# Retention attention and two feed-forward layers on one core: chunk 0 ahead of chunk 1, scaling on GpSimd, filler matmuls, another weight decode order

## The chip, the cores and the metric

The kernel runs on one core of a Trainium2 chip. The metric is the device time of one execution in microseconds (us), lower is better. Three runs of the kernel before gave 593.54, 595.24 and 596.46 us; the median is 595.24 us.

## What is computed

A causal attention with decay (a running state per head) feeds two feed-forward layers. All data are float32.

```python
# attention: B=2, H=8, S=768, D=64
for t in range(S):
    state = gamma * state + outer(k[t], v[t])
    y[t] = scale * q[t] @ state
x = y.transpose(0, 2, 1, 3).reshape(1536, 512)
# layer 1: w_in 512 x 2048, w_out 2048 x 512
h = x @ w_in
x = (max(h, 0) + alpha * min(h, 0)) @ w_out
# layer 2
h = x @ w_in2
p = a0 + a1*h + a2*h*h + a3*h**3
x = (p / (1 + |b0|*|h| + |b1|*h*h + 1e-6)) @ w_out2
```

## The kernel before

**Attention** goes in 12 chunks of 128 time steps, six for each batch entry. For a chunk `c`, `att_b` multiplies keys and queries of all heads into two PSUM banks (tiles `sc`, line L132), VectorE multiplies them with the decay mask into `s` (L136), and, when the chunk is not the first of its batch entry, ScalarE scales the queries by a constant per partition (L141, four instructions) and VectorE by the table `dq` (L142). `att_k` scales the keys `k` by a decay factor per head; for chunks below 8 that is eight ScalarE instructions (L120), for later ones one GpSimd instruction (L123). `att_c` computes `y` from `s` and `v` (L153), the chunk's own state `st` from the scaled `k` and `v` (L165), and adds the scaled `q` times the running state `R` (L177). Then `R` is copied or added to (L181, L183), and `y` is split into a high part `xh` (ScalarE, L187) and a low part `xl` (VectorE, L188). TensorE's instructions stand in a fixed order, and each of the other engines takes its own in the order written, so an instruction that waits holds everything behind it.

**The layers** are cut into 16 slices `m` of the hidden width and 3 blocks of 512 tokens. A step computes a hidden tile `h` with 12 matmuls (L309: high and low parts of `x` and of the weights), applies the activation, and multiplies it into four accumulator banks with 12 more (L326). Block 0 needs chunks 0 to 3, so the first hidden step stands behind chunk 3. The first sweep takes five slices, with the later chunks of the attention between its steps. PSUM gives four banks to a ring (`sc`, `h`, and from chunk 4 on `y` and `st`) and four to the accumulators; chunks 0 to 3 borrow those for `y` and `st`.

**Weights** arrive as 64-bit numbers, 512 KB for each half slice, and are decoded to a high part `wh` and a low part `wl`: ScalarE takes the absolute value (L253, "abs"), VectorE does three bit operations (L259, L263, L267, "word"), ScalarE rounds to `wh` (L278, "hi"), VectorE subtracts to get `wl` (L284, "lo"). The table `START` gives each half slice `(layer, m, 0 or 1)` a half step `t` at which its decode begins; "word", "hi" and "lo" follow at `t+1`, `t+2`, `t+3`. `SEQ`, the order of START, is also the order of loading. `half(t)` issues what is due at `t`; the eight entries of the list `order` (the attention of chunks 0 to 3) are the half steps -12 to -5.

**Loads** go out from SyncE's queue in the order written; each of them waits for the landing of the load eight places ahead of it. `load_next(depth)` loads weights until `depth` are in flight.

Of the kernel before, what the change touches and what calls it, by code (L numbers as in the profile page):

```python
# [11 lines left out]
ALU = mybir.AluOpType  # L12
# [19 lines left out]
def tile_fused(  # L32
# [34 lines left out]
    def drop(t):  # L67
        free.append(slot.pop(id(t))[0])
# [45 lines left out]
    def att_k(c):  # L114
        k = r8(att[c]["k"])
        if c % CPB < CPB - 1:
            o = 8 * (c % CPB)
            if c < 8:
                for h in range(8):
                    nc.scalar.mul(k[:, h, :], k[:, h, :], cst_sb[:, o + h:o + h + 1])  # L120
            else:
                dk = cst_sb[:, o:o + 8].unsqueeze(2)
                nc.gpsimd.tensor_tensor(out=k, in0=k, in1=dk.to_broadcast([P, 8, 64]), op=ALU.mult)  # L123

    def att_b(c, bank):
        a = att[c]
        ps = [bank(f"sc{c}_{e}") for e in range(2)]
        for j in range(NK):
            js = slice(j * P, (j + 1) * P)
            for e in range(2):  # L130
                es = slice(64 * e, 64 * e + 64)
                nc.tensor.matmul(ps[e][:, js], a["t"][es, js], a["q"][es, js], start=True, stop=True)  # L132
        a["s"] = alloc(f"s{c}")
        for e in range(2):
            es = slice(512 * e, 512 * e + 512)
            nc.vector.tensor_tensor(out=a["s"][:, es], in0=ps[e], in1=dm_sb[:, es], op=ALU.mult)  # L136
        if c % CPB > 0:
            for j in range(NK):
                js = slice(j * P, (j + 1) * P)
                o = 8 * CPB + 4 * (c % CPB) + j  # L140
                nc.scalar.mul(a["q"][:, js], a["q"][:, js], cst_sb[:, o:o + 1])  # L141
            nc.vector.tensor_tensor(out=a["q"], in0=a["q"], in1=dq_sb, op=ALU.mult)  # L142

    def att_c(c, ybank, pbank):
        a = att.pop(c)
# [72 lines left out]


    START = {}  # L220
    for k, e in enumerate(((1, 0), (0, 1), (2, 0), (3, 0), (1, 1), (4, 0))):
        START[(0,) + e] = k - 6
    START.update({(0, 0, 0): -12, (0, 2, 1): 0, (0, 3, 1): 2, (0, 4, 1): 4})
    for j, m in enumerate(B):
        START[0, m, 0], START[0, m, 1] = 6 + (17 * j) // 5, 8 + (17 * j) // 5
    for m in range(NF):
# [12 lines left out]
    def load_next(depth):  # L239
        while loaded[0] < len(SEQ) and loaded[0] - loaded[1] < depth:  # L240
            k = loaded[0]
            loaded[0] += 1
            l, m, n = SEQ[k]
            r = alloc(f"r{k}", U32)
            nc.sync.dma_start(out=r, in_=SRC[l][n][m].bitcast(U32))
            words = r.rearrange("p (f t) -> p f t", t=2)
            raw[k] = (words[:, :, 0], words[:, :, 1], r)
# [209 lines left out]
    N1 = NB * NF  # L457
    dec = {}
    for k, e in enumerate(SEQ):
        for o, nm in enumerate(("abs", "word", "hi", "lo")):  # L460
            dec.setdefault(START[e] + o, []).append((nm, k))

    NPRE = 12
# [1 line left out]
    def half(t, scalar_last=None, between=None):  # L465
        evs = dec.get(t, ())

        def each(nm):
            return [e[1] for e in evs if e[0] == nm]

        for e in each("abs"):
            w_abs(e)
        for e in each("hi"):
            w_hi(e)
        if scalar_last:
            scalar_last()
        for e in each("word"):
            w_word(e, 0)
        for e in each("lo"):
            w_lo(e)  # L480
        for e in each("word"):
            w_word(e, 1)
        if between:
            between()
        for e in each("word"):
            w_word(e, 2)
        if later and t % 2 == 0:
            split_x(*later.pop(0))
        load_next(0 if t < -9 else 4 if t < 2 * N1 else 2)

    with tc.manual_schedule():
        wt = alloc("wz")
# [3 lines left out]
        for _ in range(NWARM):  # L496
            nc.tensor.matmul(ps[:, 0:P], wz, wz, start=True, stop=True)
        nc.scalar.preload_act_table_set("natural_log_exp_and_others")
        drop(wt)
        for c in range(4):  # L500
            att_tiles(c)
        load_kq(0)
        nc.sync.dma_start(out=dm_sb, in_=dm)
        load_next(1)
        load_kq(1)
        nc.sync.dma_start(out=cst_sb, in_=cst)
        load_nv(0)
        load_kq(2)
        load_nv(1)
        nc.sync.dma_start(out=dq_sb, in_=dq)  # L510
        load_kq(3)
        load_nv(2)
        load_nv(3)
        load_next(2)
        nc.sync.dma_start(out=alpha_sb, in_=alpha)
        nc.sync.dma_start(out=ab_sb[:, 0:4], in_=pa.partition_broadcast(P))
        nc.sync.dma_start(out=ab_sb[:, 4:6], in_=pb.partition_broadcast(P))
        nc.vector.memset(bb_sb[:, 2:3], QC)

        order = [("b", 0), ("b", 1), ("c", 0), ("b", 2), ("c", 1), ("b", 3), ("c", 2), ("c", 3)]  # L520
        for n, (s, c) in enumerate(order):
            if s == "b":
                att_b(c, rbank)
                if c == 0:
                    att_k(c)
            else:
                att_c(c, abank(c % 2), abank(2 + c % 2))
                if c < 3:
                    att_k(c + 1)
                if c == 0:  # L530
                    att_load(4)
                    load_next(4)
                if c == 1:
                    att_load(5)
            if n == 6:
                nc.scalar.activation(bb_sb[:, 0:2], ab_sb[:, 4:6], AF.Abs)
                nc.scalar.mul(nalpha_sb, alpha_sb, -1.0)
            half(n - NPRE)
        att_b(4, rbank)
        att_k(4)  # L540


# [124 lines left out]
```

## Time and profile before

| | us |
|---|---|
| median of three runs (lowest, highest) | 595.24 (593.54, 596.46) |
| the profiled execution, device time | 595.47 |
| the profiled execution, span from first to last instruction | 593.7 |
| TensorE busy in the span | 580.1 |
| VectorE busy | 467.6 |
| ScalarE busy | 372.8 |
| GpSimd busy | 66.9 |
| mean granted TensorE clock, as a share of full speed | 0.988 |

PE is TensorE's matmuls, DVE VectorE, ACT ScalarE, POOL GpSimd, SPq SyncE's queue of loads. Times in rows are counted from the span's start. A PE group that reads x16 in the attention holds 8 matmuls of the program.

### The profile page before, as it was taken

What the parts mean: (1) busy time and instruction counts of PE and PEld (TensorE: products, weight loads), DVE (VectorE), ACT (ScalarE), POOL (GpSimd) and SP (SyncE); (2) the same over time, 40 slices, a digit from 0 to 9 for tenths busy, and PEclk for the clock granted to TensorE, in tenths of its full rate; (3) what the DMA queues carried; (4) which work ended last, traced back from release to release, by engine and by line L of the source; (5) the groups of instructions that cost most, each with busy time, mean ns of one, the idle gap of its engine ahead of it and who ended that gap; (6) DMA issues with size and microseconds to landing.
All of it is one profiled execution on the core that took longest, in us unless ns stands there. A gap on an engine that the chain in (4) does not pass through costs nothing.

```text
span 593.7 us, 8087 instructions
## 1 busy us (share of the span) xinstructions
PE 580.1 (98%) x3024; PEld 478.1 (81%) x3024; DVE 467.6 (79%) x736; ACT 372.8 (63%) x695; POOL 66.9 (11%) x53
## 2 busy tenths in 40 slices
PE   6988999999999999999999999999999999999997
PEld 6866778788888888888888888888888888888885
DVE  1786779767886255446998999999999989887886
ACT  3955655555655353444766687777787776776672
POOL 0001000000000000000000222232222222212220
PEclk8988999999999999999999999999999999999999
DMA  8997312223420111012453010111101100010101
GB/s 304 369 396 264 135 58 94 107 88 126 142 83 24 36 36 37 35 36 71 154 201 107 1 36 0 36 36 36 36 26 46 37 1 1 0 72 0 46 26 72
DMA packets 18760, 50.65 MB, mean 85 GB/s; under 512 B 2592, under 2 KB 2592, under 8 KB 18720
## 3 DMA queue, kind: packets, MB, share of 16 engines
q1 hardware_dynamic: 18720, 50.13, 24.0%
q8 instruction: 24, 0.39, 0.3%
q14 instruction: 16, 0.13, 0.1%
HBM read 46.97 MB, written 3.15 MB: 84 GB/s over the span
## 4 chain that ended last, share of the span: by engine, by line
PE 94%; DVE 2%; DMA 1%; ACT 1%; SPq 0%; issue 0%; ACTq 0%
PE h L309 44%; PE acc L326 43%; PE y L153 2%; PE sc L132 2%; PE y L177 2%; PE st L165 1%; DMA qk<-in_kT_dram 1%; DVE p L423 0%; ACT g L406 0%; DVE s L136 0%; DVE as L399 0%; DVE as L396 0%; DVE as L395 0%; DVE wl L284 0%; DVE z L259 0%
## 5 line engine op out<-in xcount | busy, mean ns | idle before, releaser
L309 PE MATMUL h<-xh,wl 128*128 128x512 f32 x384 | 150.6, 392 | 4.0 <-DVE wl L284 4.0
L309 PE MATMUL h<-xh,wh 128*128 128x512 f32 x384 | 150.8, 393 | 0.3 <-DVE xl L188 0.3
L309 PE MATMUL h<-xl,wh 128*128 128x512 f32 x384 | 150.2, 391 | 0.0
L326 PE MATMUL acc<-wh,g 128*128 128x512 f32 x384 | 125.9, 390 | 0.4 <-ACT g L406 0.4
L326 PE MATMUL acc<-g,wh 128*128 128x512 f32 x384 | 119.5, 393 | 0.0
L408 POOL TENSOR_TENSOR g<-as,g 128x512 fp32r<-128x512 f32 x46 | 63.4, 1377 | 455.5 <-PE acc L326 272.6
L309 PEld LDWEIGHTS h<-xh,wl 128*128 128x128 f32 x384 | 72.4, 189 | 19.8 <-DVE wl L284 4.9
L309 PEld LDWEIGHTS h<-xh,wh 128*128 128x128 f32 x384 | 72.3, 188 | 15.9 <-DVE xl L188 0.5
L326 PEld LDWEIGHTS acc<-wh,g 128*128 128x128 f32 x384 | 72.1, 188 | 16.1 <-ACT g L406 0.9
L326 PEld LDWEIGHTS acc<-g,wh 128*128 128x128 f32 x384 | 72.2, 189 | 15.7 <-issue 0.7
L309 PEld LDWEIGHTS h<-xl,wh 128*128 128x128 f32 x384 | 72.4, 189 | 15.2 <-DVE xl L188 0.2
L278 ACT CAST wh<-z 128x512 fp32r<-128x512 f32 x64 | 39.6, 618 | 56.9 <-DVE z L267 55.7
L326 PE MATMUL acc<-g,wl 128*128 128x512 f32 x192 | 75.0, 391 | 0.0
L326 PE MATMUL acc<-wl,g 128*128 128x512 f32 x192 | 74.7, 389 | 0.0
L350 DVE SCALAR_TENSOR_TENSOR np<-np,nalpha_sb 128x512 f32<-128x512 f32 x48 | 35.9, 748 | 39.9 <-ACT np L345 39.9
L344 ACT ACTIVATE np<-h 128x512 f32<-128x512 f32 x48 | 28.5, 594 | 45.1 <-PE h L309 45.1
L371 ACT ACTIVATE as<-h 128x512 f32<-128x512 f32 x48 | 28.6, 596 | 41.2 <-PE h L309 41.2
L377 DVE SCALAR_TENSOR_TENSOR as<-as,bb_sb,rr 128x512 f32<-128x512 f32 x48 | 37.9, 790 | 13.0 <-ACT rr L372 13.0
L360 DVE TENSOR_TENSOR g<-np,g 128x512 fp32r<-128x512 f32 x48 | 34.0, 708 | 17.4 <-ACT g L355 17.2
L284 DVE TENSOR_TENSOR wl<-z,wh 128x512 fp32r<-128x512 f32 x64 | 45.8, 716 | 0.0
L267 DVE SCALAR_TENSOR_TENSOR z<-r,z 128x512 uint32<-128x512 uint32 x64 | 44.1, 690 | 1.5
L263 DVE SCALAR_TENSOR_TENSOR z<-r,z 128x512 uint32<-128x512 uint32 x64 | 44.0, 688 | 1.0
(52 smaller groups left out, 753.0 us busy)
## 6 DMA issues: line engine op xcount, KB each, us to landing
r<-in_w1i_dram SPq DMA_DIRECT2D x16, 512.0 KB, 4.9
r<-in_w1o_dram SPq DMA_DIRECT2D x16, 512.0 KB, 4.2
r<-in_w2i_dram SPq DMA_DIRECT2D x16, 512.0 KB, 3.4
r<-in_w2o_dram SPq DMA_DIRECT2D x16, 512.0 KB, 3.3
qk<-in_qT_dram SPq DMA_DIRECT2D x12, 256.0 KB, 6.3
qk<-in_kT_dram SPq DMA_DIRECT2D x12, 256.0 KB, 6.0
kv<-in_kn_dram SPq DMA_DIRECT2D x12, 256.0 KB, 5.7
kv<-in_vn_dram SPq DMA_DIRECT2D x12, 256.0 KB, 5.7
```

The costliest lines, as they stand in the source:

```text
L263: nc.vector.scalar_tensor_tensor(out=zu, in0=lo, scalar=29, in1=zu, op0=ALU.logical_shift_right, op1=ALU.bitwise_or)
L267: nc.vector.scalar_tensor_tensor(out=zu, in0=hi, scalar=0x80000000, in1=zu, op0=ALU.bitwise_and, op1=ALU.bitwise_or)
L278: nc.scalar.copy(hi, Z[k])
L284: nc.vector.tensor_tensor(out=lo, in0=Z[k], in1=hi.bitcast(F32), op=ALU.subtract)
L309: nc.tensor.matmul(ps, w[:, ks], xs(hl, b, k, ALL), start=(n == 0), stop=(n == 11))
L326: nc.tensor.matmul(acc[0][k], a, c, start=(begin and n == 0), stop=(end != "" and n == 2))
L344: nc.scalar.activation(n, h, AF.Relu, scale=-1.0)
L350: nc.vector.scalar_tensor_tensor(out=p, in0=n, scalar=nalpha_sb[:, m:m + 1], in1=p, op0=ALU.mult, op1=ALU.add)
L360: nc.vector.tensor_tensor(out=gl, in0=p, in1=gh.bitcast(F32), op=ALU.subtract)
L371: nc.scalar.activation(s, h, AF.Square)
L377: nc.vector.scalar_tensor_tensor(out=s, in0=s, scalar=bb_sb[:, 1:2], in1=r, op0=ALU.mult, op1=ALU.add)
L408: eng.tensor_tensor(out=gl, in0=a, in1=gh.bitcast(F32), op=ALU.subtract)
```

## The change

The loads of `k` and `v` of chunk 0 go out ahead of the loads of chunk 1 and of the first weights. Chunk 0 is computed whole ahead of chunk 1. For chunks 0 to 3, GpSimd scales `k` (one instruction instead of eight on ScalarE) and multiplies `q` by `dq` (instead of VectorE). After the first three entries of `order`, 3, 2 and 3 matmuls on a tile of zeros (`keep_warm`) stand ahead of the next entry. `START` of the first sweep becomes regular, and the second weight's "word" and "hi" come a half step later, the latter together with its "lo".

```diff
-            if c < 8:
+            if 4 <= c < 8:
                 for h in range(8):
                     nc.scalar.mul(k[:, h, :], k[:, h, :], cst_sb[:, o + h:o + h + 1])
...
-            nc.vector.tensor_tensor(out=a["q"], in0=a["q"], in1=dq_sb, op=ALU.mult)
+            eng = nc.gpsimd if c < 4 else nc.vector
+            eng.tensor_tensor(out=a["q"], in0=a["q"], in1=dq_sb, op=ALU.mult)
...
-    for k, e in enumerate(((1, 0), (0, 1), (2, 0), (3, 0), (1, 1), (4, 0))):
-        START[(0,) + e] = k - 6
-    START.update({(0, 0, 0): -12, (0, 2, 1): 0, (0, 3, 1): 2, (0, 4, 1): 4})
+    for m in A:
+        START[0, m, 0], START[0, m, 1] = 2 * m - 9, 2 * m - 4
+    START[0, 0, 0] = -10
...
-        for o, nm in enumerate(("abs", "word", "hi", "lo")):
+        for o, nm in zip((0, 1, 2, 3) if k != 1 else (0, 2, 3, 3), ("abs", "word", "hi", "lo")):
...
-        load_next(0 if t < -9 else 4 if t < 2 * N1 else 2)
+        load_next(3 if t < -6 else 4 if t < 2 * N1 else 2)
...
         load_kq(0)
         nc.sync.dma_start(out=dm_sb, in_=dm)
-        load_next(1)
-        load_kq(1)
         nc.sync.dma_start(out=cst_sb, in_=cst)
         load_nv(0)
+        load_kq(1)
+        load_next(1)
         load_kq(2)
...
-        load_next(2)
+        load_next(3)
...
+        def keep_warm(cnt):
+            w = abank(3)("warm")
+            for _ in range(cnt):
+                nc.tensor.matmul(w[:, 0:P], wz, wz, start=True, stop=True)
+
-        order = [("b", 0), ("b", 1), ("c", 0), ("b", 2), ("c", 1), ("b", 3), ("c", 2), ("c", 3)]
+        order = [("b", 0), ("c", 0), ("b", 1), ("b", 2), ("c", 1), ("b", 3), ("c", 2), ("c", 3)]
         for n, (s, c) in enumerate(order):
+            if n in (1, 2, 3):
+                keep_warm((3, 2, 3)[n - 1])
             if s == "b":
+                att_k(c)
                 att_b(c, rbank)
-                if c == 0:
-                    att_k(c)
             else:
                 att_c(c, abank(c % 2), abank(2 + c % 2))
-                if c < 3:
-                    att_k(c + 1)
-                if c == 0:
-                    att_load(4)
-                    load_next(4)
-                if c == 1:
-                    att_load(5)
+                if c < 2:
+                    att_load(4 + c)
```

SyncE's queue at the program's start, before; `qk` holds q and the transposed k of a chunk, `kv` k and v, `r` a raw weight, and a chunk has one number for each (qk_95 and kv_96 are chunk 0, qk_97 and kv_98 chunk 1).

```order
L102 DMA qk_95<-in_qT_dram 128x512
L103 DMA qk_95<-in_kT_dram 128x512
L503 DMA dm_sb<-in_dm_dram 128x1024
L245 DMA r_106<-in_w1i_dram 128x1024
L102 DMA qk_97<-in_qT_dram 128x512
L103 DMA qk_97<-in_kT_dram 128x512
L506 DMA cst_sb<-in_cst_dram 128x72
L106 DMA kv_96<-in_kn_dram 128x512
L107 DMA kv_96<-in_vn_dram 128x512
L102 DMA qk_99<-in_qT_dram 128x512
```

The same place after the change.

```order
L102 DMA qk_95<-in_qT_dram 128x512
L103 DMA qk_95<-in_kT_dram 128x512
L503 DMA dm_sb<-in_dm_dram 128x1024
L504 DMA cst_sb<-in_cst_dram 128x72
L106 DMA kv_96<-in_kn_dram 128x512
L107 DMA kv_96<-in_vn_dram 128x512
L102 DMA qk_97<-in_qT_dram 128x512
L103 DMA qk_97<-in_kT_dram 128x512
L246 DMA r_111<-in_w1i_dram 128x1024
L102 DMA qk_99<-in_qT_dram 128x512
```

Three transfers, of the first weight and of chunk 1's q and transposed k, moved from ahead of chunk 0's k and v to behind them; from the last row shown on the same data have gone out.

GpSimd after the change, from its first compute instruction to its last one on chunk 3 (kv_96 to kv_102 are chunks 0 to 3, qk_97 to qk_101 chunks 1 to 3); before, none of these rows stands there, and the first is that of chunk 8, kv_637.

```order
L123 TENSOR_TENSOR kv_96<-kv_96,cst_sb 128x512
L123 TENSOR_TENSOR kv_98<-kv_98,cst_sb 128x512
L143 TENSOR_TENSOR qk_97<-qk_97,dq_sb 128x512
L123 TENSOR_TENSOR kv_100<-kv_100,cst_sb 128x512
L143 TENSOR_TENSOR qk_99<-qk_99,dq_sb 128x512
L123 TENSOR_TENSOR kv_102<-kv_102,cst_sb 128x512
L143 TENSOR_TENSOR qk_101<-qk_101,dq_sb 128x512
```

Seven instructions came to GpSimd, in an order that alternates keys and queries.

VectorE before, around the low part of the second input slice (wl_1_415) and behind chunk 4 (y_422); s_467, qk_274 and sc_0_457 belong to chunk 5.

```order
L183 TENSOR_TENSOR R<-R,st_431 128x256
L188 TENSOR_TENSOR xl_79<-y_422,xh_76 128x4x128
L136 TENSOR_TENSOR s_467<-sc_0_457,dm_sb 128x512
L136 TENSOR_TENSOR s_467<-sc_1_458,dm_sb 128x512
L142 TENSOR_TENSOR qk_274<-qk_274,dq_sb 128x512
L259 TENSOR_SCALAR z_367<-z_367 128x512
L284 TENSOR_TENSOR wl_1_415<-z_151,wh_1_414 128x512
```

The same stretch after; here wl_1_398 is that low part, qk_171 and y_406 are chunk 4, s_451 chunk 5.

```order
L143 TENSOR_TENSOR qk_171<-qk_171,dq_sb 128x512
L260 TENSOR_SCALAR z_350<-z_350 128x512
L285 TENSOR_TENSOR wl_1_398<-z_199,wh_1_397 128x512
L264 SCALAR_TENSOR_TENSOR z_350<-r_126,z_350 128x512
L268 SCALAR_TENSOR_TENSOR z_350<-r_126,z_350 128x512
L184 TENSOR_TENSOR R<-R,st_415 128x256
L189 TENSOR_TENSOR xl_79<-y_406,xh_76 128x4x128
L136 TENSOR_TENSOR s_451<-sc_0_441,dm_sb 128x512
```

The low part moved from behind chunk 5's mask product to ahead of it. The third input slice's low part moved likewise, from behind chunk 6's mask product to ahead of chunk 5's `xl`; these are the rows after (wl_2_462 is that low part, xl_79<-y_497 chunk 5, s_532 chunk 6).

```order
L351 SCALAR_TENSOR_TENSOR np_464<-np_464,nalpha_sb 128x512
L260 TENSOR_SCALAR z_459<-z_459 128x512
L285 TENSOR_TENSOR wl_2_462<-z_350,wh_2_461 128x512
L264 SCALAR_TENSOR_TENSOR z_459<-r_319,z_459 128x512
L361 TENSOR_TENSOR g_488<-np_464,g_488 128x512
L268 SCALAR_TENSOR_TENSOR z_459<-r_319,z_459 128x512
L189 TENSOR_TENSOR xl_79<-y_497,xh_76 128x4x128
L136 TENSOR_TENSOR s_532<-sc_0_522,dm_sb 128x512
```

Between the low part and chunk 6's mask product there now stand two word operations, an activation's low part `g` and chunk 5's `xl`.

## Rows read from the trace of the kernel before

**Rows 1.** The page, part 4: engines' shares of the chain that ended last.

```profile
PE 94%; DVE 2%; DMA 1%; ACT 1%; SPq 0%; issue 0%; ACTq 0%
```

**Rows 2.** Stretches: length, busy us of PE, PEld, DVE, ACT, POOL, clock, DMA, GB/s.

```profile
41.00:42.00 1.00, 1.00 (x3) 0.33 (x1) 1.00 (x2) 0.28 (x1) 0.00 (x0) 0.50 1.02 406
...
51.00:52.00 1.00, 1.00 (x4) 0.81 (x3) 1.00 (x3) 0.51 (x1) 0.00 (x0) 0.50 0.74 289
...
100.00:593.00 493.00, 489.29 (x2225) 403.78 (x2223) 398.17 (x620) 311.62 (x536) 63.35 (x46) 1.00 0.16 54
```

**Rows 3.** TensorE in order of time: start, us, instruction, [idle before it, releaser].

```profile
10.21 2.08 PE L132 MATMUL sc<-qk 64*128 64x128 f32 x16 [3.70 <-DMA qk<-in_kT_dram]
12.21 1.97 PE L153 MATMUL y<-s,kv 128*64 128x128 f32 x16
...
18.19 1.09 PE L177 MATMUL y<-qk,R 64*64 64x128 f32 x16
...
24.30 1.99 PE L165 MATMUL st<-kv 128*64 128x64 f32 x16
...
28.33 0.50 PE L309 MATMUL h<-xh,wh 128*128 128x512 f32 x1
...
38.69 0.50 PE L309 MATMUL h<-xh,wl 128*128 128x512 f32 x1 [2.07 <-DVE wl L284]
...
42.03 1.82 PE L153 MATMUL y<-s,kv 128*64 128x128 f32 x16
...
46.28 0.50 PE L309 MATMUL h<-xh,wh 128*128 128x512 f32 x1 [0.32 <-DVE xl L188]
...
48.92 0.50 PE L309 MATMUL h<-xh,wl 128*128 128x512 f32 x1 [1.91 <-DVE wl L284]
...
57.23 0.50 PE L309 MATMUL h<-xh,wh 128*128 128x512 f32 x1
```

**Rows 4.** VectorE in order of time, around the two waits and the GpSimd instructions.

```profile
28.58 0.42 DVE L259 TENSOR_SCALAR z<-z 128x512 uint32<-128x512 uint32 x1
...
37.02 0.68 DVE L142 TENSOR_TENSOR qk<-qk,dq_sb 128x512 f32<-128x512 f32 x1
...
42.69 0.69 DVE L267 SCALAR_TENSOR_TENSOR z<-r,z 128x512 uint32<-128x512 uint32 x1
45.53 0.69 DVE L188 TENSOR_TENSOR xl<-y,xh 128x512 fp32r<-128x512 f32 x1 [2.16 <-ACT xh L187]
46.14 1.28 DVE L136 TENSOR_TENSOR s<-sc,dm_sb 128x512 f32<-128x512 f32 x2
47.34 0.93 DVE L259 TENSOR_SCALAR z<-z 128x512 uint32<-128x512 uint32 x1
...
52.31 1.53 DVE L360 TENSOR_TENSOR g<-np,g 128x512 fp32r<-128x512 f32 x1
```

**Rows 5.** GpSimd in order of time.

```profile
46.94 1.04 POOL L123 TENSOR_TENSOR kv<-kv,cst_sb 128x512 f32<-128x512 f32 x1 [46.50 <-DMA kv<-in_kn_dram]
52.06 1.24 POOL L123 TENSOR_TENSOR kv<-kv,cst_sb 128x512 f32<-128x512 f32 x1 [4.08 <-DMA kv<-in_kn_dram]
```

**Rows 6.** ScalarE in order of time: the scaling of a chunk's k.

```profile
23.89 2.02 ACT L120 ACTIVATE kv<-kv,cst_sb 128x64 f32<-128x64 f32 x8
```

**Rows 7.** SyncE's queue in order of time: issue of k of chunks 0 and 2, and dq.

```profile
4.82 0.74 SPq L106 DMA_DIRECT2D kv<-in_kn_dram  x1
...
10.09 0.33 SPq L510 DMA_DIRECT2D dq_sb<-in_dq_dram  x1
...
11.58 0.33 SPq L106 DMA_DIRECT2D kv<-in_kn_dram  x1
```

**Rows 8.** The loads issued at 4.82, 10.09 and 11.58: KB, us to landing.

```profile
kv<-in_kn_dram SPq DMA_DIRECT2D x1, 256.0 KB, 6.1
...
dq_sb<-in_dq_dram SPq DMA_DIRECT2D x1, 256.0 KB, 4.8
...
kv<-in_kn_dram SPq DMA_DIRECT2D x1, 256.0 KB, 5.4
```

More of the change, by code (lines that the diff above doesn't have):

```diff
@@ L498, in tile_fused @@
         nc.scalar.preload_act_table_set("natural_log_exp_and_others")
-        drop(wt)
         for c in range(4):
@@ L538, in tile_fused @@
             half(n - NPRE)
+        drop(wt)
         att_b(4, rbank)
```

## The prediction

> **What bounds the kernel now.** The shares of the chain come first: 94% of it is TensorE [rows 1]. Read by stretch, this holds behind 100 us, where TensorE is busy 489.29 of 493 us at full granted clock [rows 2]; nothing that the diff touches stands there. What can be won or lost lies ahead of the fourth hidden step, which starts at 57.23 [rows 3]: from there on TensorE has its operands in time, so the end moves by what that start moves.
>
> TensorE in order of time shows what it loses there. It sits idle for 3.70 us until chunk 1's transposed k lands at 10.2, and then runs at half speed: 2.08 and 1.97 us for groups that take about 1.09 later. The state matmuls of chunk 3 take 1.99 us, because each needs its head's k from ScalarE. The second and third hidden steps stop after two matmuls for 2.07 and 1.91 us, until a low part `wl` comes from VectorE [all rows 3]. Behind each of those two waits the granted clock is 0.50, the lower level (1.2 GHz), for about 3.4 us [rows 2], and the work in it takes twice its time: some 1.7 us more for each.
>
> The profiled run took 595.47 us with a span of 593.7, 1.8 us around it; the median, 595.24, is 0.2 us below that run. I make the sum against the span and subtract the gain from the median.
>
> **Loads.** 1 MB (the first weight, chunk 1's q and transposed k) goes behind chunk 0's k and v. k lands at 4.82 + 6.1 = 10.9 now, dq at 14.9, chunk 2's k at 17.0 [rows 7, 8]. Between dq's issue and that k's stand chunk 3's q and k, and three quarter-MB landings in 2.1 us give about 0.7 us each. So 1 MB is 2.6 to 2.8 us: chunk 0's k lands at about 8.2, its v at 8.9. Everything from chunk 2 on has the same bytes ahead of it and lands when it did; chunk 1's v, the load ahead of dq, at 14.2. A second weight now stands ahead of chunk 4; counted on from dq (chunk 3's q and k, four quarter MB of k and v, two weights, chunk 4's q and k) chunk 4's transposed k lands at about 23.3, 1.4 later than before but ahead of its scores. Cost: none, as long as those scores don't start before 23.3.
>
> **Start of TensorE.** Chunk 0's first product still has the mask to wait for, then v: y0 starts at 9.0 instead of 12.21. The three fillers need 0.7 to 1.4 us and end by 7.9; they cover up to half of the idle time. Whether the clock holds over the rest I can't read from a row, so I let it fall: 0.9 us for each group of matmuls, as before. That costs little, because chunk 1's y needs its v at 14.2 and its scaled q later still.
>
> **GpSimd's seven instructions.** Each takes 1.04 to 1.24 [rows 5] where ScalarE takes 2.02 for a k [rows 6] and VectorE 0.68 for a q [rows 4]. ScalarE is rid of 8 us and chunk 3's state matmuls of their 1.3 us wait. But a VectorE instruction that came up beside a GpSimd instruction took 1.53 instead of 0.69 us and ended 0.5 us behind it, and one took 0.93 instead of 0.42, while the mask product beside the same GpSimd instruction kept its 1.28 [rows 4, 5]. So a VectorE operation on two SBUF tiles waits for GpSimd's end; one that reads PSUM does not. The Trainium skill (SBUF — State Buffer, "SBUF: two separate sides") calls this an exclusive lock for the whole instruction, and names as its victims VectorE operations with two SBUF inputs or in a two-port mode; the trace agrees with 1.53 us. Without that rule one could spread a slowdown of 0.5 us over all VectorE work under GpSimd, or let any VectorE work wait: the mask products of chunks 1 to 3 beside GpSimd would lose 0.5 us three times, and the sum would be 1.5 us worse.
>
> The chain, then: dq lands at 14.9, GpSimd's q1 ends at 16.0, the state term of chunk 1 starts at about 17.0 against 18.19. VectorE's three word operations on the first weight stand behind the mask products of chunks 1 and 2 (scores at 12.2 and 14.4) and begin at 16.7, three in 1.8 us if alone; the first passes, the second meets k2 (17.0 to 18.2), the third q2 (19.0 to 20.0), so they end at 20.7 instead of 18.5. R and chunk 1's xl stand behind them, so chunk 2's state term starts at 21.1. ScalarE's rounding of that weight waits for the words, q3's scaling stands behind the rounding, and GpSimd's q3 comes at 22.5 to 23.6; the first `wl` waits for that and R behind it: chunk 3's state term runs 24.7 to 25.8, chunk 4's scores to 26.9. The first hidden step starts at 26.9 against 28.33: **1.4 us won**.
>
> **The second hidden step.** Its `wl` stood behind chunk 5's mask product, which waits for TensorE; now it stands ahead. The 2.07 us go, and with them the low clock, which cost about 1.1 in the step and 0.7 in the y behind it (1.82 against 1.09) [rows 3]: **3.9 us won**. Before, the step began about 7.5 us behind the first one (two matmuls and the wait lie ahead of 38.69); so it begins at 34.4 and ends at 37.2, and three groups of 1.09 on chunks 5 and 6 end at 40.4. What is late next is the third step.
>
> **The third hidden step.** Its `wl` moved too, ahead of chunk 5's xl. But its first matmul needs a PSUM bank that this xl releases [the 0.32 us in rows 3], and xl stands at the end of a full queue. From the second weight's words on, VectorE did before, between 28.58 and 43.38, the same kinds of instruction in the same number as it must do now ahead of chunk 5's xl, with under 0.7 us idle [rows 4]: 14.1 us of work. It starts 1.27 us behind chunk 3's state term, as before, at 27.1, and is through at 41.3 to 41.9; xl adds 0.6. So the step starts at about 42.2, TensorE having waited 1.8 us from 40.4 on: a wait for xl in the place of the wait for wl. It then runs through; I let the clock fall as it did behind 1.91 us, so that ten matmuls and the output take what they took. Ten matmuls were left at 48.92; now they are left at about 42.6: 6.3 us in all, so the third step adds **1.0**.
>
> Sum: 1.4 + 3.9 + 1.0 = 6.3. I take off 0.3 for GpSimd's starts about 0.2 us behind a landing (46.94 against about 46.7): **6.0**. Span 587.7; against the median, 589.2. VectorE keeps its backlog and TensorE its lead behind the fourth step, since steps, loads and buffer waits all come earlier together.
>
> **Bounds.** If VectorE's words slip in between GpSimd's instructions, the 2.2 us between 18.5 and 20.7 come back, and 0.8 at the first `wl`: 9.0 won, 586.2. If the clock does not fall behind the third step's wait, 1.7 more, and by the sum alone 587.5. If each GpSimd instruction takes the 1.24 of its slower row, five of them in the chain cost 0.15 each, 0.7 less. The three runs spread by 1.5 us to each side.
>
> **Rivals.**
> First, **GpSimd holds VectorE less** than I count: 586.2. For it: four of its seven instructions fall where VectorE multiplies PSUM tiles. Against: the word operations begin just as k2 lands.
> Second, **GpSimd comes late to its first instruction.** Its first one now starts at 46.94 right behind its load [rows 5], long after the program's start, so the trace doesn't show what a first instruction at 8.2 costs. If k0 were ready at 13 instead of 9.4, chunk 0's state and all behind it shift by 3.6: the first hidden step comes 2.2 us later than before instead of 1.4 earlier, the two later steps still win 4.9, less 0.3: 2.4 won, 592.8. Past 15.4 the gain is gone. The Trainium skill (GPSIMD Engine Reference, "2.1 Instruction dispatch") gives about 6 us for the first call to a freshly loaded kernel; no row here shows it, as nothing is asked of GpSimd between its start and 46.9. By that figure, counted from the program's start, GpSimd would be ready ahead of 8.2 and lose nothing; counted from its first instruction it would be ready at about 14.
> Third, **slower: the alternating queue on GpSimd becomes the bound.** k1, q1, k2, q2, k3, q3 run in order, and q2 and q3 wait for ScalarE, which waits for VectorE, which GpSimd holds. I count 10 us for the six, 13.6 to 23.6, or 1.7 each with waits. Past 29.6 (2.7 us each) all the gain is gone, and at 3.3 each the time is 599. Against: the longest of the rows is 1.24.
> Fourth, **loads are the bound and nothing changes**: they run at 1.02 of their share at 41 [rows 2]. Against: counted on at 0.7 us a quarter MB from chunk 4's k at 23.3, all that the third and the fourth step need has landed by 36, and they start at 42 and 51. It gives 595.2.
>
> **Chances.** The forecast (587.2 to 591.2) 0.60; less hold 0.13; late GpSimd, with all gains of 1 to 4 us, 0.17 (the median of these is 592.8); slower 0.06; no change 0.04. A measurement here can tell 0.5%, 3 us. Faster by more: the forecast, less hold and a third of the late case, 0.79. Within: 0.15. Slower: 0.06. The range reaches from less hold (586.2) with a lucky 1.0 of the runs' spread, 585.2, to the late case with as much of it against me, 593.8.
>
> **What would show it.** Right: y0 at 9; no wait for `wl` in the second hidden step, which starts near 34.4; 1 to 2 us idle ahead of the third, released by xl; VectorE word operations of 1.5 us or more beside GpSimd at 17 to 21; the fourth step near 51. Wrong: GpSimd's first instruction long after its load's landing; a first hidden step later than 28.3; a new wait behind 60 us.

## The result and the profile after

The changed kernel takes 585.46 us (median of 4 runs, 585.32 to 585.79) against 595.05 of the kernel before (4 runs, 593.54 to 596.46): a ratio of 0.984, 95% interval 0.9815 to 0.9865. That is 9.6 us faster, where 6.0 were forecast; the time lies inside the range, 0.3 us above its lower end, and below 587.2, where the likeliest case ends. In the profiled execution the span is 583.5 us, 10.2 less than before, and the mean granted clock 1.00 instead of 0.988. Line numbers are one higher than before.

The shares of the chain are within a point or so of what they were [rows 1]: TensorE still bounds the kernel.

```profile
PE 93%; DVE 3%; ACT 2%; DMA 1%; issue 0%; ACTq 0%
```

Stretches of the kernel after (length, busy us of PE, PEld, DVE, ACT, POOL, clock, DMA, GB/s), to be read against [rows 2]:

```profile
12.00:13.00 1.00, 1.00 (x16) 0.88 (x16) 0.82 (x2) 0.88 (x3) 0.46 (x1) 1.00 1.05 404
...
41.00:42.00 1.00, 1.00 (x6) 0.80 (x5) 1.00 (x3) 1.00 (x3) 0.00 (x0) 1.00 1.05 418
...
51.00:52.00 1.00, 1.00 (x7) 0.82 (x5) 1.00 (x2) 0.96 (x2) 0.00 (x0) 1.00 1.04 399
...
100.00:583.00 483.00, 478.98 (x2133) 395.74 (x2132) 390.86 (x607) 307.06 (x525) 63.38 (x46) 1.00 0.16 54
```

Both stretches that ran at 0.50 are at 1.00, and so is every other microsecond of the first 60, whatever work now stands in it. In the kernel before a third stretch, from about 9.4 to 16.2 us, ran at 0.50:

```profile
12.00:13.00 1.00, 1.00 (x12) 0.79 (x10) 0.71 (x2) 1.00 (x6) 0.00 (x0) 0.50 1.04 387
```

Behind 100 us TensorE still is busy all but 4 us. So the gain lies at the start. TensorE of the kernel after in order of time (start, us, instruction, [idle before it, releaser]):

```profile
7.80 1.40 PE L154 MATMUL y<-s,kv 128*64 128x128 f32 x15
...
10.34 1.16 PE L132 MATMUL sc<-qk 64*128 64x128 f32 x16
...
15.27 1.09 PE L178 MATMUL y<-qk,R 64*64 64x128 f32 x16 [0.32 <-POOL qk L143]
...
18.11 1.09 PE L154 MATMUL y<-s,kv 128*64 128x128 f32 x16 [0.66 <-DVE R L184]
...
23.38 1.16 PE L132 MATMUL sc<-qk 64*128 64x128 f32 x16 [0.19 <-DMA qk<-in_kT_dram]
24.48 0.50 PE L310 MATMUL h<-xh,wh 128*128 128x512 f32 x1
...
32.10 0.50 PE L310 MATMUL h<-xh,wh 128*128 128x512 f32 x1
...
35.05 1.09 PE L154 MATMUL y<-s,kv 128*64 128x128 f32 x16
...
39.77 0.50 PE L310 MATMUL h<-xh,wh 128*128 128x512 f32 x1 [1.51 <-DVE xl L189]
...
40.34 0.40 PE L310 MATMUL h<-xh,wl 128*128 128x512 f32 x1
...
46.93 0.50 PE L310 MATMUL h<-xh,wh 128*128 128x512 f32 x1
```

Against [rows 3] the lead grows in three places. The first hidden step starts at 24.48 instead of 28.33: 3.85 us. From its start to the third matmul of the third step (48.92 before, 40.34 now) another 4.7: the wait for `wl` and the low clock of the second step are gone, and a wait of 1.51 us for `xl` stands where 1.91 us for `wl` stood. From there to the fourth step it was 8.31 us and is 6.59: 1.7 more, because the clock no longer falls. The sum is 10.3, the lead of the fourth step (57.23 to 46.93).

GpSimd of the kernel after in order of time, its whole work on chunks 0 to 3:

```profile
6.62 1.04 POOL L123 TENSOR_TENSOR kv<-kv,cst_sb 128x512 f32<-128x512 f32 x1 [6.18 <-DMA kv<-in_kn_dram]
12.54 1.04 POOL L123 TENSOR_TENSOR kv<-kv,cst_sb 128x512 f32<-128x512 f32 x1 [4.88 <-DMA kv<-in_kn_dram]
13.94 1.28 POOL L143 TENSOR_TENSOR qk<-qk,dq_sb 128x512 f32<-128x512 f32 x1 [0.35 <-ACT qk L141]
15.91 1.21 POOL L123 TENSOR_TENSOR kv<-kv,cst_sb 128x512 f32<-128x512 f32 x1 [0.70 <-DMA kv<-in_vn_dram]
17.09 1.72 POOL L143 TENSOR_TENSOR qk<-qk,dq_sb 128x512 f32<-128x512 f32 x1
18.77 1.05 POOL L123 TENSOR_TENSOR kv<-kv,cst_sb 128x512 f32<-128x512 f32 x1
19.77 1.77 POOL L143 TENSOR_TENSOR qk<-qk,dq_sb 128x512 f32<-128x512 f32 x1
```

VectorE beside it, the word operations on the first weight and the `R` behind them:

```profile
14.69 0.80 DVE L260 TENSOR_SCALAR z<-z 128x512 uint32<-128x512 uint32 x1
15.53 0.69 DVE L264 SCALAR_TENSOR_TENSOR z<-r,z 128x512 uint32<-128x512 uint32 x1
16.26 1.42 DVE L268 SCALAR_TENSOR_TENSOR z<-r,z 128x512 uint32<-128x512 uint32 x1
17.59 0.41 DVE L184 TENSOR_TENSOR R<-R,st 128x256 f32<-128x256 f32 x1
```

The first GpSimd instruction starts at 6.62, behind its load's landing (2.57 + 3.9 = 6.5, below). The q at 13.94 starts behind the landing of dq at 13.8 (below); ScalarE, which its row names, had been done with that q since 12.2. Two word operations meet a GpSimd instruction: 0.80 and 1.42 us instead of 0.42 and 0.69 [rows 4]. The three begin at 14.69 and end at 17.68, 1.2 us more than they take alone (1.8). The product `R`, which reads PSUM, keeps its 0.41.

### The profile page after: what moved, and what is told of

Its sections match the earlier page's. It is cut to its first block, busy times and chain, and to the rows that moved or that the text cites. A ratio compares the mean times of both kernels' runs of the same rounds, so it can differ in the third digit from the quotient of the medians.

```text
span 583.5 us, 8093 instructions
## 1 busy us (share of the span) xinstructions
PE 574.8 (99%) x3040; PEld 474.6 (81%) x3040; DVE 466.3 (80%) x733; ACT 365.5 (63%) x663; POOL 76.0 (13%) x60
## 4 chain that ended last, share of the span: by engine, by line
PE 93%; DVE 3%; ACT 2%; DMA 1%; issue 0%; ACTq 0%
PE h L310 44%; PE acc L327 43%; PE sc L132 2%; PE y L154 2%; PE y L178 1%; DMA qk<-in_qT_dram 1%; PE st L166 1%; PE warm L498 1%; DVE z L268 0%; DVE p L424 0%; PE warm L523 0%; ACT kv L120 0%; ACT g L407 0%; DVE as L400 0%; DVE z L264 0%
## 5 line engine op out<-in xcount | busy, mean ns | idle before, releaser
L268 DVE SCALAR_TENSOR_TENSOR z<-r,z 128x512 uint32<-128x512 uint32 x64 | 44.9, 701 | 1.5
L264 DVE SCALAR_TENSOR_TENSOR z<-r,z 128x512 uint32<-128x512 uint32 x64 | 44.9, 702 | 1.0
```

The lines of the kernel that those rows point to most:

```text
L264: nc.vector.scalar_tensor_tensor(out=zu, in0=lo, scalar=29, in1=zu, op0=ALU.logical_shift_right, op1=ALU.bitwise_or)
L268: nc.vector.scalar_tensor_tensor(out=zu, in0=hi, scalar=0x80000000, in1=zu, op0=ALU.bitwise_and, op1=ALU.bitwise_or)
```

## The experiments

Theory one: the end follows the fourth hidden step's start, and three parts bring it forward: the decode table (no waits for `wl`, no low clock), the engines, and the load and chunk order; the fillers do nothing. The rivals: one part does it all, or the fillers do by holding the clock. A first set takes one part away or adds one alone; a second goes into the terms that came out larger than forecast.

**Loads alone.** The kernel before with the new load order.

```diff
-        load_next(1)
-        load_kq(1)
         nc.sync.dma_start(out=cst_sb, in_=cst)
         load_nv(0)
+        load_kq(1)
+        load_next(1)
```

> The kernel before with the new order of loads alone (chunk 0's k and v ahead of chunk 1 and of the first weight). Theory one: in the changed kernel the mask landed at 5.5 instead of 7.4 us and chunk 1's transposed k at 8.5 instead of 10.05, and that is a gain of the load order by itself. Then TensorE's 3.70 us wait for that k shrinks to about 2.2, the first hidden step starts 1 to 1.5 us earlier (near 27), the waits of 2.07 and 1.91 us for wl stay, and the time is about 593.8. Theory two: the loads are earlier only together with the other order of computing, and the time stays at 595.

Measured: 594.58 us, ratio 1.0004 (0.9986 to 1.0023). Its first hidden step starts at 27.22, 1.1 us earlier (0.4 of that is also seen in the run with the table alone, 27.97, whose loads are the old ones); but then TensorE shows, in order of time:

```profile
37.58 0.79 PE L309 MATMUL h<-xh,wl 128*128 128x512 f32 x1 [2.07 <-DVE wl L284]
...
42.14 1.74 PE L153 MATMUL y<-s,kv 128*64 128x128 f32 x16
```

And a stretch behind that wait (columns as above, the clock third from the end):

```profile
42.00:43.00 1.00, 1.00 (x9) 0.86 (x10) 0.26 (x1) 0.00 (x0) 0.00 (x0) 0.50 1.05 391
```

The wait stands, the clock is 0.50 from 37 to past 43, about twice as long as before, and chunk 5's y comes at 42.14 (before 42.03). In that profile a later wait is shorter (1.40) and its fourth step comes 2 us earlier; the median shows none of it. The loads alone bring nothing that can be measured.

**Without fillers.** The changed kernel without the calls of `keep_warm`.

```diff
-            if n in (1, 2, 3):
-                keep_warm((3, 2, 3)[n - 1])
```

> The changed kernel without the 3, 2 and 3 filler matmuls. Theory one: the idle stretches that they cover are under 1.5 us each and the groups around them wait for loads, so nothing is lost: the granted clock stays at 1.00, the first hidden step starts at 24.3 to 24.6, and the time is 585.2 to 585.8. Theory two: the fillers keep the clock up; without them it falls to 0.50 ahead of 16 us, the groups of chunks 0 and 1 take up to 0.9 us more each, the first hidden step starts 1 to 2 us later, and the time is 586.5 to 587.5.

Measured: 585.36 us (584.85 to 585.57), as with them. TensorE waits 1.67 us ahead of chunk 0's y and 1.33 ahead of chunk 2's scores, both for loads, and the granted clock stays 1.00 behind both. The fillers have no measurable effect here.

**The old decode table** in the changed kernel.

```diff
-    for m in A:
-        START[0, m, 0], START[0, m, 1] = 2 * m - 9, 2 * m - 4
-    START[0, 0, 0] = -10
+    for k, e in enumerate(((1, 0), (0, 1), (2, 0), (3, 0), (1, 1), (4, 0))):
+        START[(0,) + e] = k - 6
+    START.update({(0, 0, 0): -10, (0, 2, 1): 0, (0, 3, 1): 2, (0, 4, 1): 4})
...
-        for o, nm in zip((0, 1, 2, 3) if k != 1 else (0, 2, 3, 3), ("abs", "word", "hi", "lo")):
+        for o, nm in zip((0, 1, 2, 3), ("abs", "word", "hi", "lo")):
```

> The changed kernel with the table START of before for the first sweep's weights (the first entry at -10, where chunk 0 now needs it) and the old spacing of the second weight. Theory one: the low parts stand behind the mask products of chunks 5 and 6 again, the second hidden step waits about 2 us for wl, the clock falls behind it and behind a wait of the third step, and 3.5 to 5.5 us of the gain are lost: 589 to 591. Theory two: VectorE and ScalarE are rid of so much work that wl is early whatever the table says, and at most 1 us is lost: 586.5.

Measured: 590.91 us (ratio to before 0.9946, 0.9919 to 0.9972), 5.4 over the changed kernel. TensorE:

```profile
24.82 0.50 PE L310 MATMUL h<-xh,wh 128*128 128x512 f32 x1
...
34.99 0.50 PE L310 MATMUL h<-xh,wl 128*128 128x512 f32 x1 [2.07 <-DVE wl L285]
...
38.30 1.82 PE L154 MATMUL y<-s,kv 128*64 128x128 f32 x16
...
44.69 0.50 PE L310 MATMUL h<-xh,wl 128*128 128x512 f32 x1 [1.40 <-DVE wl L285]
```

The first step stays early (24.82); the waits for `wl` and the y at half speed return. The table does what the prediction said.

**The table alone.** The kernel before with the change's lines of `START`, of the offsets and of `load_next`, of which a part is shown.

```diff
+    for m in A:
+        START[0, m, 0], START[0, m, 1] = 2 * m - 9, 2 * m - 4
+    START[0, 0, 0] = -10
...
+        for o, nm in zip((0, 1, 2, 3) if k != 1 else (0, 2, 3, 3), ("abs", "word", "hi", "lo")):
```

> The kernel before with the new decode table alone (loads, engines, order of the chunks as before, no fillers). Theory one (the table takes the waits for wl away by itself, and the first hidden step does not move): first hidden step at 28 to 29, no wait for wl in the second, a wait of 1 to 2 us for xl ahead of the third, clock 1.00 behind it: the 2.07 and 1.91 us of waits and both stretches of low clock go, the xl wait comes, some 5 us won: 588 to 590. Rival (the table helps only once VectorE and ScalarE have been relieved; with k and q on the old engines the changed kernel reached 591.2): 591 to 592, the first hidden step at 30 or a new wait for R ahead of it.

Measured: 590.71 us (588.86 to 591.18; ratio 0.9939, 0.9918 to 0.996): 3.3 won, between the two forecasts. The profiled run is the fastest and bears out theory one's mechanism: first hidden step at 27.97, no wait for `wl`, and on TensorE ahead of the third step

```profile
43.51 0.50 PE L309 MATMUL h<-xh,wh 128*128 128x512 f32 x1 [1.51 <-DVE xl L188]
```

The other runs are 1.3 to 2.3 us longer at a mean clock of 0.993 to 0.996, against 0.996; where they lose it, no trace shows.

**The old engines** in the changed kernel.

```diff
-            if 4 <= c < 8:
+            if c < 8:
...
-            eng = nc.gpsimd if c < 4 else nc.vector
-            eng.tensor_tensor(out=a["q"], in0=a["q"], in1=dq_sb, op=ALU.mult)
+            nc.vector.tensor_tensor(out=a["q"], in0=a["q"], in1=dq_sb, op=ALU.mult)
```

> The changed kernel with k scaled by ScalarE and q by VectorE for chunks 0 to 3, as before. Theory one: the state matmuls of chunks 2 and 3 wait for ScalarE again (0.4 and 1.3 us), VectorE has three products of 0.68 more and loses no time to GpSimd (1.2 us); the first hidden step starts 1 to 2.5 us later than 24.5 and the time is 586.5 to 588. Theory two: what GpSimd holds VectorE for is as much as it takes off, and the time stays within 0.5 of 585.5.

Measured: 591.15 us (ratio 0.9958, 0.9935 to 0.998), 5.7 over the changed kernel, more than twice what was expected; the first hidden step starts at 30.08, later than before the change. ScalarE of this run in order of time:

```profile
13.08 2.02 ACT L120 ACTIVATE kv<-kv,cst_sb 128x64 f32<-128x64 f32 x8 [1.95 <-DMA kv<-in_kn_dram]
15.01 1.26 ACT L141 ACTIVATE qk<-qk,cst_sb 128x128 f32<-128x128 f32 x4
```

And VectorE, the product of chunk 1's q that waits for it:

```profile
16.30 0.69 DVE L142 TENSOR_TENSOR qk<-qk,dq_sb 128x512 f32<-128x512 f32 x1 [3.02 <-ACT qk L141]
```

The change also wrote `att_k` ahead of `att_b`. On GpSimd chunk 2's q stands behind its k too (15.91, then 17.09, above), but no wait of TensorE comes of it; on ScalarE chunk 1's k, waiting for its load, stands ahead of chunk 1's q, for which VectorE waits 3.02 us with all else behind it. Two runs part this. First, the old engines with k written at its old places:

```diff
-                att_k(c)
                 att_b(c, rbank)
+                if c == 0:
+                    att_k(c)
             else:
                 att_c(c, abank(c % 2), abank(2 + c % 2))
+                if c < 3:
+                    att_k(c + 1)
```

> The changed kernel with k and q of chunks 0 to 3 on ScalarE and VectorE again, as in the run that lost 5.7 us, but with ScalarE's scaling of k written where the kernel before had it: behind the scores' own q scaling, one chunk ahead. Theory one (half of those 5.7 us was the place of k on ScalarE, ahead of the scaled q for which VectorE waits): first hidden step at 27 to 28.3, the rest as in the changed kernel: 588 to 589.3. Rival (it is the work itself, wherever it is written): first hidden step at 29.5 or later, and 590.5 to 591.5.

Measured: 588.71 us (588.17 to 589.42), first hidden step at 27.27. So of the 5.7 us about 2.4 belong to the place of k on ScalarE and about 3.2 to the work. Second, the changed kernel with q alone on VectorE again:

```diff
-            eng = nc.gpsimd if c < 4 else nc.vector
-            eng.tensor_tensor(out=a["q"], in0=a["q"], in1=dq_sb, op=ALU.mult)
+            nc.vector.tensor_tensor(out=a["q"], in0=a["q"], in1=dq_sb, op=ALU.mult)
```

> The changed kernel with q of chunks 1 to 3 multiplied on VectorE again; k stays on GpSimd. Theory one (with both k and q back the loss of 5.7 us came through ScalarE: it scaled k, 2.02 us each, ahead of q, so VectorE waited 1.65 to 3.02 us for the scaled q, and everything behind it came late): with k on GpSimd the scaled q comes in time, VectorE has three products of 0.69 us more ahead of the second weight's words and one GpSimd instruction less in their way: the first hidden step starts 0.5 to 1.5 us later than 24.48, and the time is 586 to 587. Rival one (it was the multiplication of q on VectorE that cost most): the first hidden step near 29 to 30 and a time of 590 to 591. Rival two (GpSimd's hold on VectorE outweighs its help): the first hidden step ahead of 24.4 and a time under 585.2.

Measured: 587.32 us (586.46 to 588.68), 1.9 over the changed kernel; theory one's direction, a little more than its bound. Its profile is of the slowest run: dq lands at 8.20 + 7.5 = 15.7, 1.9 later than in the changed kernel's, and the first hidden step starts at 27.55. VectorE's words (those of the first weight, where the expectation names the second) meet k of chunks 2 and 3 on GpSimd there:

```profile
18.20 1.27 DVE L259 TENSOR_SCALAR z<-z 128x512 uint32<-128x512 uint32 x1
19.50 1.41 DVE L263 SCALAR_TENSOR_TENSOR z<-r,z 128x512 uint32<-128x512 uint32 x1
```

**The old load and chunk order**, without fillers, engines and table changed.

```diff
-        nc.sync.dma_start(out=cst_sb, in_=cst)
-        load_nv(0)
-        load_kq(1)
         load_next(1)
+        load_kq(1)
+        nc.sync.dma_start(out=cst_sb, in_=cst)
+        load_nv(0)
...
-        order = [("b", 0), ("c", 0), ("b", 1), ("b", 2), ("c", 1), ("b", 3), ("c", 2), ("c", 3)]
+        order = [("b", 0), ("b", 1), ("c", 0), ("b", 2), ("c", 1), ("b", 3), ("c", 2), ("c", 3)]
```

> The changed kernel with the load order and the order of the first chunks of before (chunk 1's scores ahead of chunk 0's y), and without fillers; engines and decode table stay changed. Theory one (loads and order are worth about 1 us at the first hidden step, since chunk 0's k, chunk 1's q and dq land 1 to 2 us later and GpSimd and VectorE follow them): first hidden step at 25.2 to 26.2, all behind it as in the changed kernel, 586.2 to 587.2. Rival one (worth nothing: chunk 4's transposed k, at 23.4, sets the first hidden step either way): 585.2 to 585.7. Rival two (worth as much as each of the other parts): 588 or above.

Measured: 588.84 us (587.87 to 589.69), 3.4 over the changed kernel: rival two. On TensorE the wait for chunk 1's transposed k is back, and the granted clock is 0.50 from about 9.5 to 12.9:

```profile
9.61 2.08 PE L132 MATMUL sc<-qk 64*128 64x128 f32 x16 [3.05 <-DMA qk<-in_kT_dram]
```

VectorE of this run in order of time:

```profile
16.55 1.19 DVE L260 TENSOR_SCALAR z<-z 128x512 uint32<-128x512 uint32 x1
17.77 1.64 DVE L264 SCALAR_TENSOR_TENSOR z<-r,z 128x512 uint32<-128x512 uint32 x1
19.45 1.42 DVE L268 SCALAR_TENSOR_TENSOR z<-r,z 128x512 uint32<-128x512 uint32 x1
...
22.91 1.68 DVE L285 TENSOR_TENSOR wl<-z,wh 128x512 fp32r<-128x512 f32 x1
```

A stretch of the same run:

```profile
24.00:25.00 1.00, 1.00 (x18) 1.00 (x16) 1.00 (x3) 0.00 (x0) 0.04 (x1) 0.50 1.10 332
```

The same words, begun 1.9 us later, run from 16.55 to 20.87 beside k2, q2 and k3 on GpSimd: 2.5 us more than alone, and the `wl` behind them loses 1.0 to q3. TensorE waits 1.36 us for `R` ahead of 21.34, runs at 0.50 from about 23.2 on for 3.4 us, and the first hidden step starts at 28.23. Loads and chunk order were taken back together here; which of the two brings the wait and the late words, no run parts. Alone the loads brought nothing; with the scaling on GpSimd the order decides which VectorE work meets it. Read across, GpSimd's seven instructions are worth 1.9 us in the old order (590.71, the table alone, less 588.84) and 3.2 in the new (588.71 less 585.46); the first of these rests on medians of runs that spread by about 2 us, so that the difference between the two is weak.

**A longer wait.** The changed kernel with more VectorE work ahead of chunk 5's `xl`.

```diff
+        if c == 5:
+            for _ in range(2):
+                nc.vector.tensor_tensor(out=scr, in0=dm_sb[:, 0:512], in1=dm_sb[:, 512:1024], op=ALU.mult)
```

> The changed kernel with two further products of 128x512 on VectorE, on constants, just ahead of chunk 5's xl, for which the third hidden step waits 1.51 us: the wait grows by 1.2 to 1.4 us to about 2.8. Theory one (it is the length of TensorE's own wait behind which the clock falls, as it did behind 1.91 and 2.07 us in the kernel before and did not behind 1.51): granted clock 0.50 behind the wait, and a loss of 1.2 for the wait and about 1.7 for the low clock: 588.0 to 588.6. Rival (what dropped the clock in the kernel before was something else that the change took away): clock 1.00 behind the wait and a loss of the wait alone, 586.5 to 586.9.

Measured: 589.46 us (8 runs, 587.03 to 590.58). TensorE of the profiled run, of 588.13:

```profile
40.98 0.50 PE L314 MATMUL h<-xh,wh 128*128 128x512 f32 x1 [2.82 <-DVE xl L193]
...
49.73 0.50 PE L314 MATMUL h<-xh,wh 128*128 128x512 f32 x1
```

A stretch behind the wait:

```profile
43.00:44.00 1.00, 1.00 (x3) 0.78 (x3) 0.97 (x3) 0.00 (x0) 0.00 (x0) 0.50 1.04 391
```

The wait grew by 1.31 us, and the next step starts 8.75 us behind this one instead of 7.16: the low clock costs 1.6, as theory one had it. The median lies 0.9 us above theory one's range. The fastest of the 8 runs shows a mean clock of 1.0 and 587.03, about the rival's time. So at this place the clock held behind 1.5 us and fell behind 2.8 in the profiled run, and the mean clocks of six of the other seven (0.993 to 0.997, against 0.999 to 1.0 of the changed kernel) point the same way; why some runs take 590 the one trace can't say.

**q of chunks 4 and 5 on GpSimd too.**

```diff
-            eng = nc.gpsimd if c < 4 else nc.vector
+            eng = nc.gpsimd if c < 6 else nc.vector
```

> The changed kernel with q of chunks 4 and 5 on GpSimd too: two products of 0.68 us less on VectorE between the first hidden step and chunk 5's xl. Theory one (VectorE's backlog of 15 us of work sets the third hidden step, with 0.5 us idle in it): xl comes 0.6 to 1.4 us earlier, as much as the hold of GpSimd's two instructions leaves; the wait of 1.51 falls to 0.1 to 0.9 us, and the time is 584.1 to 584.9. Rival (GpSimd's hold takes all of it back, or xl waits for another engine then): the wait stays at 1.4 to 1.6 us and the time at 585.3 to 585.7, or above.

Measured: 585.94 us (585.68 to 586.32): the rival. GpSimd of this run, q of chunk 5:

```profile
33.28 1.30 POOL L143 TENSOR_TENSOR qk<-qk,dq_sb 128x512 f32<-128x512 f32 x1 [5.47 <-ACT qk L141]
```

VectorE, the word operation that meets it:

```profile
33.62 1.24 DVE L260 TENSOR_SCALAR z<-z 128x512 uint32<-128x512 uint32 x1
```

TensorE, the start of the third hidden step:

```profile
40.38 0.50 PE L310 MATMUL h<-xh,wh 128*128 128x512 f32 x1 [1.74 <-DVE xl L189]
```

The hold of this word operation (0.82 us) takes back more than the one product saved (0.68); what the other saved became a wait of 0.81 us for ScalarE's rounding, ahead of a `wl` that comes no earlier.

**Words behind the wait.** The changed kernel with the fourth slice's "word" and "hi" a half step later.

```diff
-        for o, nm in zip((0, 1, 2, 3) if k != 1 else (0, 2, 3, 3), ("abs", "word", "hi", "lo")):
+        for o, nm in zip((0, 1, 2, 3) if k not in (1, 4) else (0, 2, 3, 3), ("abs", "word", "hi", "lo")):
```

> The changed kernel with the three word operations on the fourth slice's input weight (1.8 us of VectorE work) a half step later, behind chunk 5's xl instead of ahead of it, and its rounding a half step later too. Theory one (the wait of 1.51 us ahead of the third hidden step is VectorE's backlog): xl comes at about 37.9 instead of 39.03, bound by ScalarE's xh, which ends at 37.8; the third step waits 0.2 to 0.5 us, the fourth starts at about 45.8 instead of 46.93, and the time is 584.0 to 584.7. Rival (the backlog is only moved: the low part of the fourth slice, or one of the accumulator matmuls, comes late instead): a wait of about 1 us at one of these ahead of the fifth hidden step, and 585.2 to 586.

Measured: 584.12 us (583.88 to 584.38; ratio to before 0.9834, 0.9797 to 0.9871), below every run of the changed kernel and where theory one had it. TensorE:

```profile
38.75 0.50 PE L310 MATMUL h<-xh,wh 128*128 128x512 f32 x1 [0.32 <-DVE xl L189]
...
45.92 0.50 PE L310 MATMUL h<-xh,wh 128*128 128x512 f32 x1
```

The wait was VectorE's backlog, as the prediction had it, and work that nobody waits for yet could be taken out of it.

All together, in us:

| kernel | median | against the changed kernel | fourth step starts (profiled run) |
|---|---|---|---|
| before, in four sets of runs | 593.9 to 595.1 | +8.4 to +9.6 | 57.23 |
| loads alone | 594.58 | +9.1 | 55.18 |
| table alone | 590.71 | +5.2 | 50.66 |
| old engines | 591.15 | +5.7 | 52.81 |
| old engines, k at its old place | 588.71 | +3.2 | 50.03 |
| old table | 590.91 | +5.4 | 51.38 |
| old order | 588.84 | +3.4 | 50.95 |
| q on VectorE | 587.32 | +1.9 | 50.28 |
| longer wait | 589.46 | +4.0 | 49.73 |
| q of chunks 4 and 5 on GpSimd | 585.94 | +0.5 | 47.55 |
| no fillers | 585.36 | -0.1 | 46.45 |
| changed | 585.46 | 0 | 46.93 |
| words behind | 584.12 | -1.3 | 45.92 |

In every profiled run the span ends 536.4 to 536.7 us behind the fourth step's start (593.7 - 57.23, 583.5 - 46.93, 582.6 - 45.92): the prediction's frame holds. The changed kernel stands in one of the four sets and its variants in the other three, so differences of well under 1 us say nothing; that of the words behind, 1.3, is borne out by its trace. Order, table and engines (these with k at its old place) taken away one at a time cost 3.4 + 5.4 + 3.2 = 12.0 us, more than the whole gain of 9.6: the parts help one another. The engines alone, or the chunk order alone, in the kernel before were not run.

## Why the prediction was right in sign and 4.2 us short

By the spans the change won 10.2 us against the 6.0 forecast, 4.2 more; by the medians 9.6, 3.6 more. Of the signs that the prediction named, no wait for `wl` in the second step and a wait of 1 to 2 us for `xl` ahead of the third were seen; chunk 0's y, the words and the fourth step all came earlier than it said (7.80, 14.69 and 46.93).

**The frame and the second step: right.** The wait for `wl` and the low clock went, for 3.9 us, as forecast: from the first step to chunk 5's y it was 13.7 us (42.03 - 28.33) and is 10.57, 3.1 less, and that y itself takes 1.09 instead of 1.82.

**The third step's wait: right.** Forecast 1.8 us for `xl` in the place of the wait for `wl`; measured 1.51, and the run with the words behind it showed its cause.

**The clock behind that wait: wrong, 1.7 us.** The forecast let it fall as behind 1.91 us and kept the other case as a bound of 1.7 us. It stayed at 1.00 behind 1.51, and behind 1.74 in the run with q of chunks 4 and 5 on GpSimd; behind 2.82 it fell. The step that failed carried the low clock over from a longer wait. Its price was right: 1.7 here, 1.6 in the run with the longer wait.

**The start: right in direction, mis-sized by 2.45 us.** The first hidden step was forecast at 26.9 and came at 24.48. The chain broke in three terms. First, the loads: y0 was forecast at 9.0, from landings at 8.2 and 8.9, and came at 7.80. The landings of the kernel after (KB, us from issue) for the mask, issued at 1.63, chunk 0's k at 2.57, dq at 7.14 and chunk 2's k at 10.44:

```profile
dm_sb<-in_dm_dram SPq DMA_DIRECT2D x1, 512.0 KB, 3.9
...
kv<-in_kn_dram SPq DMA_DIRECT2D x1, 256.0 KB, 3.9
...
dq_sb<-in_dq_dram SPq DMA_DIRECT2D x1, 256.0 KB, 6.7
...
kv<-in_kn_dram SPq DMA_DIRECT2D x1, 256.0 KB, 5.4
```

They land at 5.5, 6.5, 13.8 and 15.8; the last two landed at 14.9 and 17.0 before [rows 7, 8], and by the bytes ahead of them should not have moved. Part of that is no effect of the order: over the ten runs with this start of the queue the mask lands anywhere from 5.5 to 6.9 and dq from 13.8 to 15.7, with the same loads ahead of them. And the profile that the prediction was read from was a late one: with the old order of loads the mask landed at 6.6 and 6.3 and dq at 14.3 in two more runs (the table alone, the old order), where it had 7.4 and 14.9. Second, the clock: the forecast let it fall at the start, at up to 0.9 us a group, and held that this costs little. It stayed at 1.00, with the fillers and without, and the scores of chunks 1 and 2 came at 10.34 and 12.30 instead of 12.2 and 14.4; 1.2 us of that is y0's lead, the rest goes with the clock. The mask products and the words behind them followed. Third, GpSimd's hold: the words were forecast from 16.7 to 20.7, with 2.2 us lost to GpSimd; they ran from 14.69 to 17.68 and lost 1.2. The mechanism is the one the prediction named: each word that was held ended 0.3 to 0.6 us behind GpSimd's instruction (15.49 behind 15.22, 17.68 behind 17.12). Only the meeting moved, since the words started before k2 and not with it; with the old order they did end at 20.87, after 2.5 us of hold, about as forecast for the change. The operations that wait are not only those with two input tiles: the shift (L260) works on one tile in place and took 0.80, 1.24 and 1.27 us beside GpSimd, against 0.42 alone. The 0.3 us taken off for late starts of GpSimd is not seen either: it starts 0.1 us behind the landings at 6.5 and 15.8.

1.7 + 2.45 + 0.3, less 0.15 in the third step, make the 4.3 us by which the fourth step came earlier than forecast.

The Trainium skill (SBUF — State Buffer, "SBUF: two separate sides") has the lock go to whichever instruction starts first, with the other fully blocked. The trace agrees in both directions: q2 came up at 17.09 while the word operation begun at 16.26 still ran to 17.68, and itself took 1.72 us, where q1 took 1.28; the word operation in its turn had been held by k2, which ended at 17.12.

**The rivals.** GpSimd is not late to its first instruction (6.62), and its queue is no bound: k1 to q3 take 9.0 us, from 12.54 to 21.54, against 10 counted. Neither do the loads stop the rest: chunk 4's transposed k, forecast at 23.3, comes at about 23.4, and its scores wait 0.19 us for it. That load is now close to a floor for the first hidden step: in the runs with the old table and with the longer wait the same scores wait 0.40 and 0.29 for it. "Less hold", at 586.2, was nearest to the time, but only in part to what happened: of the 2.2 us of hold 1.0 came back, and the loads and the clock brought the rest. That the time lies inside the range is partly luck, as the range did not hold two good cases at once: less hold (9.0) and a clock that stays (1.7) together would have been 584.5, below its end.

## What to carry to other kernels

When work moves to GpSimd, list the VectorE operations that touch only SBUF tiles and will run beside it: the same seven instructions were worth 3.2 us here in one order and about 1.9 in the other, and two more of them nothing. A wait's price is its length plus what TensorE's clock does behind it, so look for the granted clock at each wait of a microsecond or more, and price both cases. Before counting on a load's landing or on a clock from one profile, look at how far they move from run to run. Parts of a change that each gain nothing or little alone may gain together, so take parts away from the whole as well as adding them one by one.

## What the runs showed of the hardware beyond this

- The granted clock does not follow from a wait's length alone. It stayed 1.00 behind waits of 1.51, 1.67 and 1.74 us, fell to 0.50 behind 1.91, 2.07 and 2.82, but stayed 1.00 behind 1.86 us for a load ahead of chunk 0's y (the run with the longer wait, at 8.38), behind 1.90 and 2.18 us for `R` among the attention's matmuls (q on VectorE, at 22.11; the old engines, at 22.90), and fell in the run with the old order around waits of 1.36 and 0.16. What decides there stays open.
- The first loads of one and the same queue land 1.4 to 1.9 us apart from run to run (the mask, dq), and chunk 0's y starts anywhere from 7.80 to 8.54 in the nine of them that compute chunk 0 first.
- GpSimd's product of 128x512 took 1.04 us alone and up to 1.77 beside VectorE (1.85 in the run with q of chunks 4 and 5).
